# First FFN layer of five groups in 11 instead of 12 products of halves, with the attention one part ahead

One core of a Trainium2 chip. The metric is device microseconds of one execution, median over several; lower is better.

## The reference

Gated linear attention, then a feed-forward layer with a squared ReLU, all FP32 (the weights arrive as 64-bit floats and are converted on the chip).

```python
# q, k, v, alpha: (4, 8, 768, 48)
for t in range(S):
    state = alpha[:, :, t, :, None] * state + einsum('bhd,bhe->bhde', k[:, :, t], v[:, :, t])
    y[:, :, t] = einsum('bhd,bhde->bhe', q[:, :, t], state)
x = y.transpose(0, 2, 1, 3).reshape(3072, 384)
h = maximum(x @ w_in, 0)          # w_in: (384, 2048)
out = (h * h) @ w_out             # w_out: (2048, 384)
```

## The kernel before

The tokens go through in six groups of four blocks of 128. While TensorE does the FFN of group g (`units`), the attention of group g+1 is woven in: each block has four parts (`stages`), and each of the 16 slots of a group takes one attention part and then one sixteenth of the FFN. Groups two to six already use Strassen's seven products for the second layer; the first layer is the plain one. PSUM has four banks for the FFN (`ps_ffn`) and four for the attention.

```python
def ffn_in(g, j):                      # one hidden tile: 128 of 2048 columns, 512 tokens
    ...                                # cut: hid[j // 2] from its pool
    ps = ps_ffn.tile([128, GB * C], FP32, tag="f", name="h")
    for kk in range(KM):               # KM = 3
        nc.tensor.matmul(out=ps, lhsT=w[:, kk, c0 : c0 + 128], rhs=xT[g][:, kk, :],
                         start=(kk == 0), stop=(kk == KM - 1))
    r = p2.tile([128, GB * C], FP32, tag="r", name="r")
    nc.scalar.activation(out=r, in_=ps, func=AF.Relu)
    ...                                # cut: square on ScalarE (first group) or VectorE,
                                       # and four half sums of the hidden tiles on VectorE

stages = [(aT, ln, sn, eb, ei), (qT, mq, kT, mk), (sc, am, kr, kc), (kv, sm, y, ev, st)]
# TensorE: aT qT kT sc kr kv y    ScalarE: ln eb ei kc ev    VectorE: sn mq mk am sm st

for slot in range(NS):                 # NS = 16
    i, s = divmod(slot, len(stages))
    n = (g + 1) * GB + i
    if n < NBLK:
        for f in stages[s]:
            f(n)
    next_weights()
    ...
    while units and done * NS < total * (slot + 1):
        f, args = units.pop(0)
        f(*args)
        done += cost[f]
```

`ev` is twelve ScalarE copies of y out of PSUM into `xT`; `sn` is a scan on VectorE; `eb` and `ei` are exponentials of its result on ScalarE.

## Time and profile before

| | before |
|---|---|
| median (range) of the first runs | 630.0 us (629.78 to 630.14) |
| span of the profiled run (itself one of 632.01 us) | 630.2 us |
| TensorE matmul busy | 616.5 us (98%) |
| VectorE, ScalarE busy | 305.3 us (48%), 224.9 us (36%) |
| first layer, all groups | 576 matmul instructions of 512 columns |

TensorE is the row to read: nearly all of the span, and the chain that ended last is 89% TensorE. The lines themselves stand in the prediction. An FP32 matmul is two instructions here, each with its weight load. "Busy" of a matmul includes a modelled tail, so I measure rates by the distance of starts.

### The profile page before, as it was taken

The numbers are of one execution on the slowest core, as the hardware profiler recorded it, in microseconds if no ns is written. First come the engines' busy times: TensorE is split into PE (matmuls) and PEld (weight loads), VectorE is DVE, ScalarE is ACT, GpSimd is POOL, SyncE is SP. The second block draws the span as 40 slices with busy tenths as digits, with TensorE's granted clock in tenths as the row PEclk, the third lists the DMA queues.
The fourth block names the chain that finished last, engine by engine and source line by source line (L and its number), as shares of the span: only waits on it lengthen the run. The fifth ranks groups of instructions, "written<-read, shape, count | busy, mean of one in ns | idle before, by whom it ended". The sixth has DMA issues, their size and how long they took to land.

```text
span 630.2 us, 8103 instructions
## 1 busy us (share of the span) xinstructions
PE 616.5 (98%) x3284; PEld 438.9 (70%) x3284; DVE 305.3 (48%) x484; ACT 224.9 (36%) x533; POOL 3.8 (1%) x18
## 2 busy tenths in 40 slices
PE   7979999999999999999999999999999999999997
PEld 5745456665556998555899655799854599844797
DVE  5777768674865323555423357523255442145301
ACT  3867784525334123243230443422324403222100
POOL 2000000000000000000000000000000000000000
PEclk8979999999999999999999999999999999999999
DMA  9983755508020201711300802110262000100001
GB/s 155 263 184 102 176 146 127 101 1 143 8 51 14 37 1 54 98 23 29 51 1 25 126 1 50 29 24 2 73 78 50 1 1 1 50 2 0 1 0 51
DMA packets 108709, 36.70 MB, mean 58 GB/s; under 512 B 100480, under 2 KB 103552, under 8 KB 108672
## 3 DMA queue, kind: packets, MB, share of 16 engines
q1 hardware_dynamic: 108672, 36.18, 29.7%
q8 instruction: 26, 0.43, 0.3%
q14 instruction: 11, 0.09, 0.0%
HBM read 31.46 MB, written 4.72 MB: 57 GB/s over the span
## 4 chain that ended last, share of the span: by engine, by line
PE 89%; ACT 5%; DVE 4%; issue 1%; DVEq 0%
PE h L399 36%; PE o L455 29%; PE o L423 6%; PE sc L261 4%; PE y L325 3%; PE y L318 3%; PE kv L290 2%; ACT xT L345 2%; PE kr L279 2%; PE qT L211 1%; PE aT L211 1%; PE kT L211 1%; ACT hid L407 1%; ACT power L137 1%; DVE power L147 1%
## 5 line engine op out<-in xcount | busy, mean ns | idle before, releaser
L399 PE MATMUL h<-xT,w_in 128*128 128x512 f32 x576 | 258.2, 599 | 1.5 <-DVE w_in L154 1.5
L399 PEld LDWEIGHTS h<-xT,w_in 128*128 128x128 f32 x576 | 106.7, 191 | 121.6 <-issue 119.3
L409 DVE TENSOR_TENSOR hid<-r 128x512 f32<-128x512 f32 x80 | 54.8, 691 | 114.7 <-ACT r L404 114.7
L345 ACT COPY xT<-y 32x128 f32<-32x128 f32 (+3 forms) x282 | 72.9, 259 | 102.6 <-PE y L325 97.8
L404 ACT ACTIVATE r<-h 128x512 f32<-128x512 f32 x96 | 56.4, 592 | 114.0 <-PE h L399 113.8
L455 PE MATMUL o<-w_out,hid 128*128 128x192 f32 x480 | 82.0, 327 | 0.0
L455 PEld LDWEIGHTS o<-w_out,hid 128*128 128x128 f32 x480 | 78.1, 190 | 3.1 <-issue 3.1
L455 PE MATMUL o<-t,s 128*128 128x192 f32 x320 | 55.1, 326 | 0.0
L225 DVE TENSOR_TENSOR_SCAN la<-again,la 128x512 f32<-128x512 f32 x24 | 29.3, 1222 | 51.4 <-ACT la L220 51.4
L455 PEld LDWEIGHTS o<-t,s 128*128 128x128 f32 x320 | 52.1, 190 | 0.1
L269 DVE COPY_PREDICATED am<-causal,sc 128x512 f32<-128x512 uint32 x48 | 32.4, 730 | 28.5 <-PE sc L261 28.4
L423 PE MATMUL o<-w_out,hid 128*128 128x384 f32 x128 | 42.9, 489 | 0.3 <-DVE w_out L154 0.3
L423 PEld LDWEIGHTS o<-w_out,hid 128*128 128x128 f32 x128 | 23.7, 190 | 15.7 <-DVE w_out L154 0.5
L261 PEld LDWEIGHTS sc<-qs,ks 48*128 48x128 f32 x384 | 23.8, 191 | 11.2 <-issue 7.4
L284 ACT ACTIVATE kc<-kr 128x512 f32<-128x512 f32 x20 | 11.9, 596 | 49.8 <-PE kr L279 49.8
L234 ACT ACTIVATE b<-la 128x512 f32<-128x512 f32 x24 | 15.1, 630 | 38.7 <-DVE la L225 38.7
L261 PE MATMUL sc<-qs,ks 48*128 48x128 f32 x384 | 28.5, 289 | 0.0
L455 PE MATMUL o<-w_out,s 128*128 128x192 f32 x160 | 27.9, 329 | 0.0
L325 PE MATMUL y<-am,v_in 128*48 128x128 f32 (+1 forms) x384 | 26.5, 278 | 1.4 <-ACT xT L345 1.4
L455 PE MATMUL o<-t,hid 128*128 128x192 f32 x160 | 27.6, 327 | 0.0
L455 PEld LDWEIGHTS o<-w_out,s 128*128 128x128 f32 x160 | 26.0, 190 | 0.7 <-issue 0.7
L455 PEld LDWEIGHTS o<-t,hid 128*128 128x128 f32 x160 | 26.0, 190 | 0.1
(65 smaller groups left out, 498.4 us busy)
## 6 DMA issues: line engine op xcount, KB each, us to landing
raw<-in_moe_w_in_dram SPq DMA_DIRECT2D x8, 768.0 KB, 5.4
raw<-in_moe_w_out_dram SPq DMA_DIRECT2D x8, 768.0 KB, 4.3
a_in<-in_alpha_dram SPq DMA_DIRECT2D x24, 192.0 KB, 4.1
q_in<-in_q_dram SPq DMA_DIRECT2D x24, 192.0 KB, 3.9
k_in<-in_k_dram SPq DMA_DIRECT2D x24, 192.0 KB, 4.4
v_in<-in_v_dram SPq DMA_DIRECT2D x24, 192.0 KB, 4.5
out_dram<-osb SPq DMA_DIRECT2D x24, 192.0 KB, 2.0
```

The lines of the kernel that those rows point to most:

```text
L211: nc.tensor.transpose(out=ps[:, p, :], in_=rows[:, 128 * p : 128 * (p + 1)], identity=ident)
L225: nc.vector.tensor_tensor_scan(out=la.rearrange("a p t -> a (p t)"), data0=again.rearrange("a p t -> a (p t)"), data1=la.rearrange("a p t ...
L261: nc.tensor.matmul(out=ps[e][:, p, :], lhsT=blk[n]["ks"][rows, p, :], rhs=blk[n]["qs"][rows, p, :], start=True, stop=True,)
L269: nc.vector.copy_predicated(out=am_t[n % NAM][:, e], mask=causal.bitcast(U32).unsqueeze(1).to_broadcast([128, NP, C]), data=ps,)
L318: nc.tensor.matmul(out=ys[p // per][:, p % per, :], lhsT=s_t[n % B][:, p, :], rhs=blk[n]["qs"][:, p, :], start=(p % per == 0), stop=False, ...
L325: nc.tensor.matmul(out=ys[p // per][64 * e : 64 * e + D + G * e, p % per, :], lhsT=v_in[:, (2 * p + e) * D - G * e : (2 * p + e + 1) * D], ...
L345: copy(out=xT[g][to : to + m, kk, t * C : (t + 1) * C], in_=ys[p // per][r : r + m, p % per, :],)
L399: nc.tensor.matmul(out=ps, lhsT=w[:, kk, c0 : c0 + 128], rhs=xT[g][:, kk, :], start=(kk == 0), stop=(kk == KM - 1),)
L404: nc.scalar.activation(out=r, in_=ps, func=AF.Relu)
L409: nc.vector.tensor_tensor(out=h, in0=r, in1=r, op=ALU.mult)
L423: nc.tensor.matmul(out=acc[t][:, 0:DM], lhsT=hid[i][:, j, t * C : (t + 1) * C], rhs=w_out[i][:, j, :], start=(i == 0 and j == 0), stop=(i ...
L455: nc.tensor.matmul(out=acc[k][:, t, :], lhsT=lhs[:, j, t * C : (t + 1) * C], rhs=rhs[:, j, :], start=(first and r + j + t == 0), stop=(r = ...
```

## The change

The three row tiles of the contraction (384 = 3 x 128) are taken as two and one. On the first two, Strassen's algorithm over halves (two halves of the hidden columns, two halves of the tokens) needs 7 products of 256 columns instead of 8; the third tile adds its 4. So 11 instead of 12 per pair of hidden tiles. The products go into four PSUM banks, A to D. Strassen's scheme needs running sums of them: ScalarE copies the first product in A to u1, VectorE adds B to it (u2) and C to that (u3). The second products of a pair add to A, C and D, and each must wait until its bank has been read. The sums of the weights are made once, those of x once a group; for this x must be complete earlier, so the attention runs one part ahead. The second layer keeps its products, in another order, and makes its hidden sums in place.

```diff
+    def ffn_in_pair(g, j, part):
+        ...
+        def product(k, *pairs):        # accumulators A, B, C, D: the four banks
+            ...                        # start only at a bank's first matmul of the pair
+        if part == 0:
+            nc.scalar.copy(out=u1, in_=product("A", (a11, b11)))
+            add(u2, product("B", (s2, t2)), u1)
+            add(u3, product("C", (s3, t3), (a23, b32)), u2)
+            add(h2[:, HT : 2 * HT], product("D", (s1, t1)), u3)
+        else:
+            c11 = product("A", (a12, b21), (a13, b31))
+            nc.scalar.activation(out=h1[:, 0:HT], in_=c11, func=AF.Relu)
+            add(h2[:, 0:HT], product("C", (a22, t4), (a23, d3)), u2)
+            add(h1[:, HT : 2 * HT], product("D", (s4, b22), (a13, b32)), u2)
+            ...                        # relu and squares, one hidden sum per two pairs
-            units = [(ffn_in, (g, j)) for j in order]
+            units = [(ffn_in_pair, (g, j, part)) for j in range(NJ // 2) for part in range(2)]
-    PRODUCTS = (("1", 0), ("6", 1), ("2", 0), ("7", 2), ("5", 3), ("4", 2), ("3", 3))
+    PRODUCTS = (("1", 0), ("5", 3), ("6", 1), ("7", 2), ("2", 0), ("4", 2), ("3", 3))
+    stage_ahead(NS)
     for slot in range(NS):
-            if n < NBLK:
-                for f in stages[s]:
-                    f(n)
+            stage_ahead(NS * (g + 1) + slot + 1)
             next_weights()
+            ...                        # cut: weight sums, sums of x in the last slot
```

(Cuts are marked with dots; the moves of helper functions are left out.)

More of the change, by code (lines that the diff above doesn't have):

```diff
@@ L360, in st, with combine, sum_w_in @@
         blk[n].clear()
-    hid, acc, sums = {}, {}, {}
+    hid, acc, ws, xs, sums = {}, {}, {}, {}, {}
     HT, HM, NR2 = GB * C // 2, DM // 2, NJ // 4
-    t1, t2, t4 = (kept(f"t{i}_", NR2, [128, 2, HM]) for i in (1, 2, 4))
-    def sum_weights(r):
+    def combine(steps):
+        for o, x, op, z in steps:
+            nc.vector.tensor_tensor(out=o, in0=x, in1=z, op=op)
+    def sum_w_in(r):
+        if r % 2 == 0:
+            ws["tile"] = raw_pool.tile([128, 6, 256], FP32, tag="raw", name="ws")
+        s1, s2, s4 = ws[r] = [ws["tile"][:, 3 * (r % 2) + i, :] for i in range(3)]
+        a11, a12 = w_in[r][:, 0, :], w_in[r][:, 1, :]
+        a21, a22 = w_in[NR2 + r][:, 0, :], w_in[NR2 + r][:, 1, :]
+        combine((
+            (s1, a21, ALU.add, a22), (s2, s1, ALU.subtract, a11),
+            (a21, a11, ALU.subtract, a21), (s4, a12, ALU.subtract, s2),
+        ))
@@ L371, in sum_weights, with sum_w_out @@
+    tsum = [kept(f"t{i}_", NR2, [128, 2, HM]) for i in (1, 2, 4)]
+    def sum_w_out(i):
+        i, r = divmod(i, NR2)
+        t1, t2, t4 = (t[r] for t in tsum)
         b11, b12 = w_out[r][:, :, 0:HM], w_out[r][:, :, HM:DM]
         b21, b22 = w_out[NR2 + r][:, :, 0:HM], w_out[NR2 + r][:, :, HM:DM]
-        for o, x, z in ((t1, b12, b11), (t2, b22, t1), (t4, b21, t2), (None, b22, b12)):
-            nc.vector.tensor_tensor(
-                out=o[r] if o else b12, in0=x, in1=z if not isinstance(z, list) else z[r],
-                op=ALU.subtract,
-            )
+        o, x, z = ((t1, b12, b11), (t2, b22, t1), (b12, b22, b12), (t4, b21, t2))[i]
+        combine(((o, x, ALU.subtract, z),))
@@ new lines, in sum_x @@
+    def sum_x(g):
+        if not xs:
+            a = raw_pool.tile([128, 3, 2, HT], FP32, tag="raw", name="s012")
+            z = raw_pool.tile([128, 6, HT], FP32, tag="raw", name="s3x")
+            sums.update({r: a[:, r] for r in range(3)})
+            sums[3] = z[:, 0:2, :]
+            xs[0] = [z[:, 2 + i, :] for i in range(4)]
+        t1, t2, t4, d3 = xs[0]
+        (b11, b12), (b21, b22), (b31, b32) = (
+            (xT[g][:, kk, 0:HT], xT[g][:, kk, HT : 2 * HT]) for kk in range(KM)
+        )
+        combine((
+            (t1, b12, ALU.subtract, b11), (t2, b22, ALU.subtract, t1),
+            (b12, b22, ALU.subtract, b12), (t4, b21, ALU.subtract, t2),
+            (d3, b31, ALU.subtract, b32),
+        ))
@@ L379, in halves @@
     def halves(j):
         return hid[j][:, :, 0:HT], hid[j][:, :, HT : 2 * HT]
-    def sum_hidden(r):
-        a11, a21 = halves(r)
-        a12, a22 = halves(NR2 + r)
-        s124 = raw_pool.tile([128, 3, 2, HT], FP32, tag="raw", name="s124")
-        s1, s2, s4 = sums[r] = s124[:, 0], s124[:, 1], s124[:, 2]
-        for o, x, op, z in (
-            (s1, a21, ALU.add, a22), (s2, s1, ALU.subtract, a11),
-            (a21, a11, ALU.subtract, a21), (s4, a12, ALU.subtract, s2),
-        ):
-            nc.vector.tensor_tensor(out=o, in0=x, in1=z, op=op)
@@ L393, in ffn_in, with hidden_tile @@
-    def ffn_in(g, j):
+    def hidden_tile(j):
         if j % 2 == 0:
             hid[j // 2] = hid_pool.tile([128, 2, GB * C], FP32, tag="hid", name="hid")
+        return hid[j // 2][:, j % 2, :]
+    def ffn_in(g, j):
         w, c0 = w_in[j * NW // NJ], j % (NJ // NW) * 128
@@ L402, in ffn_in @@
             )
-        r = p2.tile([128, GB * C], FP32, tag="r", name="r")
+        r = p2.tile([128, 3, HT], FP32, tag="u", name="r")[:, 0:2, :]
         nc.scalar.activation(out=r, in_=ps, func=AF.Relu)
-        h = hid[j // 2][:, j % 2, :]
-        if g == 0:
-            nc.scalar.activation(out=h, in_=r, func=AF.Square)
-        else:
-            nc.vector.tensor_tensor(out=h, in0=r, in1=r, op=ALU.mult)
-            if j >= NJ // 2 and j % 2:
-                sum_hidden(j // 2 - NR2)
+        nc.scalar.activation(out=hidden_tile(j), in_=r, func=AF.Square)
@@ new lines, in ffn_in_pair, with add @@
+    def ffn_in_pair(g, j, part):
+        r, cols = j // 2, slice(j % 2 * 128, j % 2 * 128 + 128)
+        a11, a12, a13 = (w_in[r][:, kk, cols] for kk in range(KM))
+        s3, a22, a23 = (w_in[NR2 + r][:, kk, cols] for kk in range(KM))
+        s1, s2, s4 = (x[:, cols] for x in ws[r])
+        t1, t2, t4, d3 = xs[0]
+        (b11, t3), (b21, b22), (b31, b32) = (
+            (xT[g][:, kk, 0:HT], xT[g][:, kk, HT : 2 * HT]) for kk in range(KM)
+        )
+        def product(k, *pairs):
+            first = k not in acc
+            if first:
+                acc[k] = ps_ffn.tile([128, GB * C], FP32, tag="f", name="h")[:, 0:HT]
+            for i, (a, b) in enumerate(pairs):
+                nc.tensor.matmul(
+                    out=acc[k], lhsT=a, rhs=b, start=(first and i == 0),
+                    stop=(i == len(pairs) - 1), skip_group_check=True,
+                )
+            return acc[k]
+        def add(o, x, z):
+            nc.vector.tensor_tensor(out=o, in0=x, in1=z, op=ALU.add)
+        if part == 0:
+            acc["h"] = hidden_tile(j), hidden_tile(j + NJ // 2)
+            acc["u"] = p2.tile([128, 3, HT], FP32, tag="u", name="u")
+        h1, h2 = acc["h"]
+        u1, u2, u3 = (acc["u"][:, i, :] for i in range(3))
+        if part == 0:
+            nc.scalar.copy(out=u1, in_=product("A", (a11, b11)))
+            add(u2, product("B", (s2, t2)), u1)
+            add(u3, product("C", (s3, t3), (a23, b32)), u2)
+            add(h2[:, HT : 2 * HT], product("D", (s1, t1)), u3)
+        else:
+            c11 = product("A", (a12, b21), (a13, b31))
+            nc.scalar.activation(out=h1[:, 0:HT], in_=c11, func=AF.Relu)
+            add(h2[:, 0:HT], product("C", (a22, t4), (a23, d3)), u2)
+            add(h1[:, HT : 2 * HT], product("D", (s4, b22), (a13, b32)), u2)
+            for k in "ABCD":
+                acc.pop(k)
+            nc.vector.scalar_tensor_tensor(
+                out=h2, in0=h2, scalar=0.0, in1=h2, op0=ALU.max, op1=ALU.mult
+            )
+            nc.scalar.activation(out=h1[:, HT : 2 * HT], in_=h1[:, HT : 2 * HT], func=AF.Relu)
+            nc.scalar.activation(out=h1, in_=h1, func=AF.Square)
+            if j % 2:
+                a21, a22 = halves(r)[1], halves(NR2 + r)[1]
+                combine(((sums[r], a21, ALU.add, a22),))
@@ L444, in ffn_product @@
             acc[k] = ps_ffn.tile([128, 2, HM], FP32, tag="f", name="o")
-        (a11, s3), (a12, a22) = halves(r), halves(NR2 + r)
-        s1, s2, s4 = sums[r]
+        (a11, a21), (a12, a22) = halves(r), halves(NR2 + r)
+        s = sums[r]
+        t1, t2, t4 = (t[r] for t in tsum)
         b11, t3 = w_out[r][:, :, 0:HM], w_out[r][:, :, HM:DM]
@@ L449, in ffn_product @@
         lhs, rhs = {
-            "1": (a11, b11), "2": (a12, b21), "3": (s4, b22), "4": (a22, t4[r]),
-            "5": (s1, t1[r]), "6": (s2, t2[r]), "7": (s3, t3),
+            "1": (a11, b11), "2": (a12, b21), "3": (s, b22), "4": (a22, t4),
+            "5": (s, t1), "6": (s, t2), "7": (a21, t3),
         }[name]
@@ L459, in ffn_product @@
                 )
+        if name == "5":
+            combine(((s, s, ALU.subtract, a11), (a21, a11, ALU.subtract, a21)))
+        elif name == "6":
+            combine(((s, a12, ALU.subtract, s),))
         if r < NR2 - 1:
@@ L467, in ffn_product @@
             nc.scalar.activation(out=acc["u1"], in_=acc[k], func=AF.Copy)
+        elif name == "5":
+            pass
         elif name in "67":
@@ L470, in ffn_product @@
             if new == "u3":
-                acc[new] = p2.tile([128, 2, HM], FP32, tag=new, name=new, bufs=1)
+                acc[new] = acc["out", 1][:, :, HM:DM]
             nc.vector.tensor_tensor(out=acc[new], in0=acc[k], in1=acc[u], op=ALU.add)
+            if new == "u3":
+                nc.vector.tensor_tensor(
+                    out=acc[new], in0=acc[3], in1=acc[new], op=ALU.add
+                )
         else:
-            h, m, u = {"2": (0, 0, None), "5": (1, 1, "u3"), "4": (1, 0, "u2"), "3": (0, 1, "u2")}[name]
+            h, m, u = {"2": (0, 0, None), "4": (1, 0, "u2"), "3": (0, 1, "u2")}[name]
             o = acc["out", h][:, :, m * HM : (m + 1) * HM]
@@ L482, in ffn_product @@
                     store(g, 2 * h + t, acc["out", h][:, t, :])
+            if name == "3":
+                acc.clear()
     stages = [(aT, ln, sn, eb, ei), (qT, mq, kT, mk), (sc, am, kr, kc), (kv, sm, y, ev, st)]
@@ L502, with stage_ahead @@
         steps[f](*([int(rest[0]), rest[1:]] if f == "load" else map(int, rest)))
+    def stage_ahead(i):
+        n, k = divmod(i, len(stages))
+        if n < NBLK:
+            for f in stages[k]:
+                f(n)
+            if k == 0 and n + 1 < NBLK:
+                load(n + 1)
     NS = GB * len(stages)
+    stage_ahead(NS)
     for g in range(NBLK // GB):
         if g:
-            order = [j for r in range(NR2) for i in (r, NR2 + r) for j in (2 * i, 2 * i + 1)]
-            units = [(ffn_in, (g, j)) for j in order]
+            units = [(ffn_in_pair, (g, j, part)) for j in range(NJ // 2) for part in range(2)]
             units += [(ffn_product, (g, i, r)) for i in range(len(PRODUCTS)) for r in range(NR2)]
@@ L513 @@
             units += [(ffn_out, (g, t, i)) for i in range(NW) for t in range(GB)]
-        cost = {ffn_in: KM * GB * C, ffn_out: NJ // NW * DM, ffn_product: 4 * HM}
+        cost = {
+            ffn_in: KM * GB * C, ffn_in_pair: 11 * HT // 2, ffn_out: NJ // NW * DM,
+            ffn_product: 4 * HM,
+        }
         total = sum(cost[f] for f, _ in units)
@@ L517 @@
         for slot in range(NS):
-            i, s = divmod(slot, len(stages))
-            n = (g + 1) * GB + i
-            if n < NBLK:
-                for f in stages[s]:
-                    f(n)
-            next_weights()
-            if g == 1 and slot < NR2:
-                sum_weights(slot)
-            if s == 0 and n + 1 < NBLK:
-                load(n + 1)
+            stage_ahead(NS * (g + 1) + slot + 1)
+            next_weights()
+            if 0 <= g * NS + slot - (NS - 3) < NR2:
+                sum_w_in(g * NS + slot - (NS - 3))
+            if g == 1 and 3 <= slot < 11:
+                sum_w_out(2 * slot - 6)
+                sum_w_out(2 * slot - 5)
+            if slot == NS - 1 and g + 1 < NBLK // GB:
+                sum_x(g + 1)
             while units and done * NS < total * (slot + 1):
```

## The prediction

> **What bounds the kernel now.** I read the busy table and the slices first, then the groups of instructions, then the time line of one stretch in which the first FFN layer and the attention are interleaved.
>
> ```profile
> PE 616.5 (98%) x3284; PEld 438.9 (70%) x3284; DVE 305.3 (48%) x484; ACT 224.9 (36%) x533; POOL 3.8 (1%) x18
> PE   7979999999999999999999999999999999999997
> PEclk8979999999999999999999999999999999999999
> ```
> ```profile
> 60.00:600.00 540.00, 539.33 (x2811) 378.46 (x2812) 260.51 (x411) 186.64 (x449) 0.00 (x0) 1.00 0.24 46
> ```
>
> TensorE is the bound: from 60 to 600 us it shows 539.33 us of work in 540 us (last line, busy times of PE, PEld, DVE and ACT in a window). A busy matmul is not yet one at full rate, so I also took the distance from one matmul's start to the next out of the trace: 0.429 us for a 512-column instruction, 0.1625 us for 192 columns, 0.109 us for 128. After 60 us these distances add up to the time with under 1 us of rest. So TensorE streams without stalls, the two vector engines are half idle, and any column removed is time gained, as long as no stall comes in. Any new stall is time lost, in full.
>
> ```profile
> L399 PE MATMUL h<-xT,w_in 128*128 128x512 f32 x576 | 258.2, 599 | 1.5 <-DVE w_in L154 1.5
> ...
> L404 ACT ACTIVATE r<-h 128x512 f32<-128x512 f32 x96 | 56.4, 592 | 114.0 <-PE h L399 113.8
> ```
> ```profile
> 270.33 3.29 ACT L345 COPY xT<-y 32x128 f32<-32x128 f32 x12 [2.21 <-PE y L325]
> ...
> 273.65 0.60 ACT L404 ACTIVATE r<-h 128x512 f32<-128x512 f32 x1
> ...
> 276.18 0.59 ACT L220 ACTIVATE la<-aT 128x512 f32<-128x512 f32 x1
> ...
> 279.58 1.22 DVE L225 TENSOR_TENSOR_SCAN la<-again,la 128x512 f32<-128x512 f32 x1
> ...
> 280.83 0.63 ACT L234 ACTIVATE b<-la 128x512 f32<-128x512 f32 x1 [4.06 <-DVE la L225]
> ...
> 281.36 0.61 ACT L238 ACTIVATE inv<-la 128x512 f32<-128x512 f32 x1
> ...
> 281.88 1.06 ACT L404 ACTIVATE r<-h 128x512 f32<-128x512 f32 x2
> ```
>
> The first block has two groups, the second lines of the time line (start, length). They show what the reader should keep in mind: ScalarE takes its work strictly in program order. When an attention part puts `ln, exp, exp` or twelve copies (3.29 us) ahead, the ReLU of a finished FFN tile waits: here the tile was ready near 279.1 and its ReLU began at 281.88. TensorE didn't notice, because one tile takes it 6 x 0.429 = 2.57 us and four PSUM buffers let it run three tiles (7.7 us) ahead. That slack is what the change spends.
>
> **What the Trainium skill says.** "TensorE: Matmul & The Clock Gate", section "Back-to-back issue gap", gives an isolated spacing of N/2.4 + 2.5 ns. This trace has twice that per instruction for FP32 (0.429 us at 512), which fits N/1.2 + 2.4 ns, also at 192 and 128; an estimate for 256 columns is thus 0.2158 us. The same page, "Step-by-step: what each phase is for", says matmuls stay in program order and only weight loads are pulled ahead, so a matmul that waits holds up all behind it; the trace agrees (kr, then kv, both waited with the rest behind them). "PSUM — Partial Sum Buffer", section "Engine vs sequencer instructions", says that ScalarE and VectorE are strict first-in first-out; the 281.88 line agrees. The first page's "What's actually happening" has the clock halved after an idle window of about 3.4 us. Here the clock record has windows of 3.413 us, and halves after windows that held 1.12 us (8.1 to 11.5) and 1.04 us (32.0 to 35.4) of streaming; it stays full after one with 1.57 us. So a gap of over some 2 us inside one window may be enough.
>
> **The change part by part.** *Matmuls.* In each of groups two to six, 8 pairs of hidden tiles took 2 x 3 products of 512 columns, at two instructions each: 5 x 8 x 12 = 480 instructions, 480 x 0.429 = 205.9 us. Now each pair has 11 products of 256 columns: 5 x 8 x 22 = 880 instructions x 0.2158 = 189.9 us. Gain **16.0 us**. Weight loads double, but at 128-column matmuls loads keep up with 0.109 us spacing, so they stay hidden. The second layer keeps its 28 x 4 products per group.
>
> *Vector work.* Off the path as a sum: per pair VectorE has five adds of 256 columns (about 0.42 us each, an estimate from 0.691 at 512, 0.558 at 384 and 0.354 at 192) and one of 512 (0.69); before, two squares (1.38) and half of four sums (1.38). ScalarE has three short ones (0.37) and a square (0.63) for two ReLUs (1.18). Both are far under TensorE's 4.75 us a pair.
>
> *Order.* This is the core. A pair's products go A, B, C, C, D (2.16 us), then again into the same accumulators A, A, C, C, D, D (2.59 us). Between them ScalarE must copy A (u1), and VectorE must add B (u2), C (u3), D, each needing the one before. The second A overwrites what the copy reads, so TensorE waits for it: the slack is 1.73 us from the end of A, instead of 7.7 us. The built order puts exactly one attention part and then one pair in each slot, and that part's ScalarE and VectorE work goes ahead of u1 and u2. I work it out for each kind, with 0 as the moment TensorE has issued the previous pair's last product. Handoffs of 0.035 us, and 0.165 us for the matmul's tail, are from the trace. The previous pair's tail is: D lands 0.17, VectorE add to 0.62, its ReLU-square of the other half to 1.23; ScalarE ReLU to 1.03, square to 1.69.
>
> Pair after aT (two per group, four groups): `ln` 1.60 to 2.19, scan 2.23 to 3.45, `exp` 3.48 to 4.11, second `exp` to 4.63, u1 to 4.91; the matmul restarts at about 5.0. TensorE had aT (0.44) and the first five products (2.16), so it stood ready at 2.60. Stall **2.4 us** x 8 = 19.2.
>
> Pair after kv and y (two per group, four groups): these take TensorE 2.9 us; the twelve copies begin when y lands, 3.0, and last to 6.3; u1 to 6.62, restart 6.75. TensorE was ready at 2.9 + 2.16 = 5.06. Stall **1.7 us** x 8 = 13.6.
>
> Pair after qT and kT in the middle of the layer (one per group, four groups): VectorE has the hidden sum to 2.42, then mq and mk to 3.61, u2 to 3.97, u3 to 4.42. The second C needs u3, and TensorE is there at 0.87 + 2.16 + 0.86 = 3.9. Stall 0.65 x 4 = 2.6.
>
> Pair after sc and kr: kc on ScalarE to 2.39, u1 to 2.67, TensorE there at 3.75; u3 is ready at 3.93 and needed at 4.6. No stall.
>
> Group two also carries the weight sums on VectorE: some 1.5 us. Group six has no attention: u1 is ready when needed, and the sum after every second pair makes u3 late by some 0.5 us: with the group's start about 2 us.
>
> *Clock.* A gap of 2.4 us lying nearly whole in one 3.413 us window leaves it with about 1 us of streaming; the chance is about (3.41 - 2.4 + 0.4)/3.41 = 0.4. Each halved window costs 1.7 us: 8 x 0.4 x 1.7 = 5.5, **say 6 us**; the shorter stalls leave over 1.6 us and shouldn't do it.
>
> *Attention one part ahead.* It frees the slot in which the sums of x are made and takes away two waits of 0.5 us at 72 and 100 us; in group one it moves mq and mk ahead of a weight conversion. Net about 0.
>
> *Second layer.* Its in-place sums come after product 5: 4 x 1.4 us on VectorE, and product 6 needs the last of them about 9 us after product 5 began; they finish near 7, or 8.4 with an attention part between. No stall.
>
> Sum: 630.0 - 16.0 + 19.2 + 13.6 + 2.6 + 1.5 + 2.0 + 6.0 = 658.9; I say **658 us**, slower.
>
> **The rivals.** (a) *Work bound*: the stalls hide, and the 16 us come through: 614 us, 2.5% faster. For it speaks that TensorE is at 98% and the vector engines at about half. Against it: an average says nothing on latency, and ScalarE's queue alone keeps u1 back by 3 to 4 us in half of the attention slots. With half of my stalls it would be about 635. (b) *Stalls without the clock*: the waits come as worked out, but the clock stays full: 653 us. (c) *VectorE as the new bound*: if the 256-column adds cost like 512-column ones, a pair has 5 x 0.69 + 0.69 + 0.35 = 4.5 us, with attention more than TensorE's slot in places; the pairs after qT would stall by 2 us more, and the second C, not the second A, would be the usual wait: about 670 us. The near straight line through 192, 384 and 512 speaks against it. (d) *Weight loads bind at 256 columns*: 880 x 0.24 would eat the gain; the 192-column group at 0.1625 speaks against it.
>
> **Range and chances.** The surest term is the 16.0 us; the stalls of 39 us may be off by a third (26 to 50), the clock from 0 to 10. Together 642 to 672 us, 8 times in 10. Slower by over 2% means over 642.6; within 2% needs stalls of some 4 to 28 us in all, which would take my handoffs to be wrong in kind; faster needs nearly none. Chances: faster 0.04, same 0.07, slower 0.89.
>
> **What would show it.** Right: 880 first-layer matmuls with starts 0.216 us apart where nothing waits; TensorE idle after 60 us in pieces of about 2.4 us (released by the ScalarE copy u) in the pairs after aT, about 1.7 us after kv and y, none after sc; some half-clock windows right after the former; PE busy below 95%. Group six without attention should gain about 1 us over its old length. Wrong: PE still near 98% and the span near 614 (the copy isn't what the second A waits for, or ScalarE is free sooner); waits ended by VectorE's u3 as the larger share (rival c); even spacing of 0.24 us or more without waits (rival d); stalls in the second layer.

## The result

| | before | after |
|---|---|---|
| median (range) | 629.89 us (629.24 to 630.14) | 666.31 us (662.04 to 667.1) |
| span of the profiled run | 630.2 us | 664.0 us |
| mean granted clock of that run | 0.991 | 0.982 |

All outputs are right. The ratio is 1.0566 (95% interval 1.052 to 1.0612): 5.7% slower. Ratios are the mean time of one kernel's fast runs over that of the other's of the same rounds, so not quite the ratio of the medians quoted.

The page of the changed kernel, its busy table and two rows of the slices, and then the window of 60 to 600 us (busy times of PE, PEld, DVE, ACT):

```profile
PE 615.7 (93%) x3684; PEld 515.7 (78%) x3684; DVE 375.3 (57%) x685; ACT 247.9 (37%) x613; POOL 3.8 (1%) x18
PE   7799999998888999988899979799998989999997
PEclk9989999999898999989999989999998989999999
```
```profile
60.00:600.00 540.00, 505.63 (x3023) 426.45 (x3022) 306.54 (x565) 197.87 (x497) 0.00 (x0) 0.98 0.22 45
```

Where TensorE had 539.33 us of work in 540 us it now has 505.63: gaps of 34 us. And the clock row, full after the start before, now has single slices at 8 in the middle. Who TensorE waited for, in the view of waits (total us, times, longest):

```profile
PE h L449 <- ACT u L464: 29.1, 16, 2.2
PE h L449 <- DVE u L456: 3.9, 8, 1.5
```

Sixteen waits for one instruction, the ScalarE copy u1; this is what half of the 32 pairs of groups two to five do. (This view counts idle time from a matmul's modelled end; by distances of starts the sixteen are eight of 1.6 us and eight of 2.4 us, 31.7 us in all.) The time line shows one of each kind. First a pair after kv and y (start, length):

```profile
273.88 3.28 ACT L345 COPY xT<-y 32x128 f32<-32x128 f32 x12 [1.29 <-PE y L325]
277.18 0.37 ACT L464 COPY u<-h 128x256 f32<-128x256 f32 x1
```
```profile
275.59 0.59 PE L449 MATMUL h<-s3x,ws 128*128 128x256 f32 x2
277.61 1.13 PE L449 MATMUL h<-xT,w_in 128*128 128x256 f32 x4 [1.43 <-ACT u L464]
```

A's first product was done near 274.5, but u1 could not start before 277.18, behind the twelve copies. The line at 275.59 is D, the last product that needs no u1; then TensorE waits to 277.61. The next pair, after aT:

```profile
280.43 0.60 PE L211 MATMUL aT<-ident,a_in 128*128 128x128 f32 x4
...
281.54 0.63 ACT L479 ACTIVATE hid<-hid 128x512 f32<-128x512 f32 x1
...
282.07 0.58 ACT L220 ACTIVATE la<-aT 128x512 f32<-128x512 f32 x1
...
282.60 0.59 PE L449 MATMUL h<-s3x,ws 128*128 128x256 f32 x2
282.68 1.22 DVE L225 TENSOR_TENSOR_SCAN la<-again,la 128x512 f32<-128x512 f32 x1 [1.03 <-ACT la L220]
283.94 0.63 ACT L234 ACTIVATE b<-la 128x512 f32<-128x512 f32 x1 [1.29 <-DVE la L225]
284.48 0.61 ACT L238 ACTIVATE inv<-la 128x512 f32<-128x512 f32 x1
285.00 0.35 ACT L464 COPY u<-h 128x256 f32<-128x256 f32 x1
...
285.40 1.74 PE L449 MATMUL h<-xT,w_in 128*128 128x256 f32 x4 [2.21 <-ACT u L464]
```

It is the same queue again: ScalarE sits idle for 1.29 us with u1's input ready, since the exponential ahead of u1 waits for VectorE's scan. At 285.79 the clock is halved for one window, so the four matmuls from 285.40 take 1.74 us instead of the 1.13 us of those at 277.61.

### The profile page after: what moved, and what is told of

Same layout as the page of the kernel before. It is cut to its first block, busy times and chain, and to the rows that moved or that the text cites. A ratio compares the mean times of both kernels' runs of the same rounds, so it can differ in the third digit from the quotient of the medians.

```text
span 664.0 us, 9283 instructions
## 1 busy us (share of the span) xinstructions
PE 615.7 (93%) x3684; PEld 515.7 (78%) x3684; DVE 375.3 (57%) x685; ACT 247.9 (37%) x613; POOL 3.8 (1%) x18
## 4 chain that ended last, share of the span: by engine, by line
PE 76%; ACT 13%; DVE 8%; issue 2%; DVEq 0%
PE o L528 28%; PE h L449 25%; PE o L494 6%; ACT xT L345 6%; PE sc L261 4%; PE y L325 3%; PE y L318 2%; DVE la L225 2%; PE kv L290 2%; PE kr L279 2%; PE qT L211 1%; PE kT L211 1%; ACT b L234 1%; ACT la L220 1%; ACT hid L479 1%
## 5 line engine op out<-in xcount | busy, mean ns | idle before, releaser
L449 PE MATMUL h<-xT,w_in 128*128 128x256 f32 x480 | 135.1, 394 | 29.1 <-ACT u L464 29.1
L456 DVE TENSOR_TENSOR hid<-h,u 128x256 f32<-128x256 f32 x120 | 51.0, 425 | 64.6 <-PE h L449 60.4
L456 DVE TENSOR_TENSOR u<-h,u 128x256 f32<-128x256 f32 x80 | 33.9, 424 | 44.1 <-ACT u L464 36.6
L449 PE MATMUL h<-s3x,w_in 128*128 128x256 f32 x160 | 48.4, 429 | 3.9 <-DVE u L456 3.9
L478 ACT ACTIVATE hid<-hid 128x256 f32<-128x256 f32 x40 | 16.7, 417 | 87.5 <-DVE hid L456 87.5
L449 PE MATMUL h<-s3x,ws 128*128 128x256 f32 x160 | 47.6, 379 | 0.0
L425 PE MATMUL h<-xT,w_in 128*128 128x512 f32 x96 | 42.9, 596 | 2.4 <-DVE w_in L154 2.4
L449 PEld LDWEIGHTS h<-s3x,w_in 128*128 128x128 f32 x160 | 31.2, 207 | 15.5 <-DVE u L456 11.5
L470 ACT ACTIVATE hid<-h 128x256 f32<-128x256 f32 x40 | 15.3, 383 | 67.5 <-PE h L449 67.5
L449 PEld LDWEIGHTS h<-s3x,ws 128*128 128x128 f32 x160 | 30.4, 190 | 4.1
```

What stands on the lines that cost most here:

```text
L449: nc.tensor.matmul(out=acc[k], lhsT=a, rhs=b, start=(first and i == 0), stop=(i == len(pairs) - 1), skip_group_check=True,)
L456: nc.vector.tensor_tensor(out=o, in0=x, in1=z, op=ALU.add)
L470: nc.scalar.activation(out=h1[:, 0:HT], in_=c11, func=AF.Relu)
L478: nc.scalar.activation(out=h1[:, HT : 2 * HT], in_=h1[:, HT : 2 * HT], func=AF.Relu)
```

## The experiments

Two batches, on two chips, each beside runs of the kernel before (medians 630.15 and 630.28 us). All edits are to the changed kernel, unless said.

### e1: all vector work of the attention behind the first half of a pair

In a slot the attention part's matmuls stay where they are; its ScalarE and VectorE instructions are emitted after part 0 of the pair.

```diff
+    TENSOR = (aT, qT, kT, sc, kr, kv, y)
+    LATE = (0, 1, 2, 3)
     def stage_ahead(i, pair_next=False):
             for f in stages[k]:
-                f(n)
+                if pair_next and k in LATE and f not in TENSOR:
+                    later.append((f, n))
+                else:
+                    f(n)
     ...
                 f, args = units.pop(0)
                 f(*args)
+                for h, n in later:
+                    h(n)
+                later = []
```

> The changed kernel, with the ScalarE and VectorE work of each attention part moved in program order behind the first half (A, B, C, C, D and u1, u2, u3) of the pair that follows it. No instruction is added or taken away. Theory (queue order: u1 waits behind the attention part's work, and the second A waits for u1): the sixteen stalls of 1.6 and 2.4 us (32 us), most of the stalls after qT (about 5 us) and all clock drops in the interleaved groups (six halved windows, 10 us) go; span about 630 - 16 + 3 = 617 us, at most 622. Rival 1 (256-column instructions, doubled weight loads or the longer accumulation groups cost the time): they are all still there, so the time stays near 664. Rival 2 (VectorE is the new bound): its work is the same, so at most a small part goes, above 650.

Measured: 619.86 us (616.55 to 620.1), ratio 0.9813 (0.978 to 0.9846). The view of waits has no wait for ScalarE's u1 left, and four short ones for VectorE's u:

```profile
PE h L449 <- DVE u L456: 1.0, 4, 0.4
```

The time line of ScalarE in the pair after aT:

```profile
269.42 0.35 ACT L464 COPY u<-h 128x256 f32<-128x256 f32 x1
269.68 0.60 ACT L220 ACTIVATE la<-aT 128x512 f32<-128x512 f32 x1
272.46 0.63 ACT L234 ACTIVATE b<-la 128x512 f32<-128x512 f32 x1 [2.19 <-DVE la L225]
273.00 0.61 ACT L238 ACTIVATE inv<-la 128x512 f32<-128x512 f32 x1
```

ScalarE still waits for the scan, longer than before (2.19 us), but u1 is through, and nobody needs the exponentials yet. The same instructions on the same engines, in another order, make the 664.0 us span 617.9 us. (Against the kernel before, the gain of 1.9% is clear of noise, but whether it reaches 2% is not: the interval spans 0.98.) That rules out the narrower matmuls, the doubled weight loads and VectorE's load as the cause of the loss (rivals c and d of the prediction). Distances of starts agree: the median between 256-column instructions is 0.216 us in the changed kernel too.

### e2 and e3: one kind of part alone

e2 is e1 with `LATE = (0,)` (ln, scan, two exps), e3 with `LATE = (3,)` (kv, y, twelve copies).

> As the run before, for the parts with ln, scan and two exps alone. Theory: eight stalls of 2.4 us go (19.2 us), and since only these left a clock window with under 1.2 us of streaming, all six halved windows go too (10.2 us): about 664 - 29 = 635 us, with the 1.6 us stalls after kv and y still there and the clock at full throughout the interleaved groups. If the clock drops have another cause (the 1.6 us stalls, or the mean load), some stay and the time is 638 to 645.

> As e1, for the parts with kv, y and the twelve copies alone. Theory: eight stalls of 1.6 us go (12.7 us), the 2.4 us stalls and about six halved clock windows stay: about 664 - 13 = 651 us. Rival: if the 1.6 us stalls had a share in the halved windows, these fall in number and the time is under 648.

Measured: e2 637.64 us (636.33 to 638.82), ratio 1.0106; e3 649.8 us (645.15 to 654.03), ratio 1.0287. Waits of e2, then of e3:

```profile
PE h L449 <- ACT u L464: 11.4, 8, 1.4
PE h L449 <- DVE u L456: 4.5, 8, 1.6
```
```profile
PE h L449 <- ACT u L464: 17.7, 8, 2.2
PE h L449 <- DVE u L456: 3.9, 8, 1.5
```

Each move took away its own eight waits and left the other eight. (e2 is 2.6 us over its figure; its profiled run has four halved windows at the start where that of the changed kernel has one, which may be a part of it.) And the clock, the same row of the slices of e2, then of e3:

```profile
PEclk8979999999999999999999999999999999999999
```
```profile
PEclk8979999999898999989999999899998999999999
```

With the short stalls alone (e2) no window is halved after the start; with the long ones alone (e3) six are. So in these runs the clock follows the 2.4 us stalls and not the 1.6 us ones. How many windows fall changes from run to run: e3's four timed runs went from 645.15 us at a mean clock of 0.992 to 654.03 us at 0.974, the changed kernel's from 662.04 us at 0.987 to 667.1 us at 0.977. This fits the scatter of these two, 5 to 9 us where the kernel before scatters by under 3; that the count depends on where the windows lie is argued, since only one run of each was traced.

### e4: the kernel before with the attention one part ahead alone

```diff
+    stage_ahead(NS)
             for slot in range(NS):
-            if n < NBLK:
-                for f in stages[s]:
-                    f(n)
+            stage_ahead(NS * (g + 1) + slot + 1)
```

> The kernel before, with only the attention one part ahead (12 products, 512 columns, old order of the second layer). Theory: this part of the change is neutral, 629 to 631 us, perhaps 1.6 us more from a wait for a weight conversion near 65 us. Rival: the shift itself puts attention work at worse places and costs several us or more.

Measured: 630.56 us (630.49 to 630.75), ratio 0.9995 (0.9973 to 1.0017). This part of the change is neutral. The wait for a weight conversion near 66 us (1.6 us) and one of 0.5 us near 93 us did come.

### e6: the second half in the order C, D, A

```diff
-            c11 = product("A", (a12, b21), (a13, b31))
-            nc.scalar.activation(out=h1[:, 0:HT], in_=c11, func=AF.Relu)
             add(h2[:, 0:HT], product("C", (a22, t4), (a23, d3)), u2)
             add(h1[:, HT : 2 * HT], product("D", (s4, b22), (a13, b32)), u2)
+            c11 = product("A", (a12, b21), (a13, b31))
+            nc.scalar.activation(out=h1[:, 0:HT], in_=c11, func=AF.Relu)
```

> The changed kernel with the second half of a pair in the order C, C, D, D, A, A instead of A, A, C, C, D, D. Rival: the wait is for the reuse of bank A while ScalarE reads it; then moving the second A to the end takes the sixteen stalls away, about 625 us. Theory: the wait is for the chain that begins at u1, and A is only where it is first felt; the second C then waits for u3, 0.95 us later (u2 and u3 at 0.42 us each and handoffs), so the stalls grow to about 3.3 and 2.5 us, other pairs get small ones, more clock windows are halved: 685 to 705 us.

Measured: 701.38 us (698.11 to 702.72), ratio 1.1129. The stalls are 3.2 us after aT and 2.6 us after kv and y, and the one releaser is now a VectorE add. In the pair after aT near 295 us the two adds u2 and u3 end at 295.32 us and TensorE restarts at 295.38 us, with the second C, so it is u3, the add that reads C:

```profile
PE h L449 <- DVE u L456: 55.5, 29, 3.0
```

So the bank that TensorE comes to first is only where the wait is felt. What is late is the chain u1, u2, u3, and the later its link, the longer the wait. The author's order, A first, is the best of these two.

### e7: u1 on VectorE

```diff
-            nc.scalar.copy(out=u1, in_=product("A", (a11, b11)))
+            nc.vector.tensor_copy(out=u1, in_=product("A", (a11, b11)))
```

> The changed kernel with one line changed: the copy u1 is made by VectorE (a 256-column copy, some 0.4 us) instead of ScalarE; the attention's work stays where it is. Theory (u1 waits in ScalarE's queue): after kv and y VectorE isn't held up by the twelve copies, so those eight stalls of 1.6 us go altogether; after aT VectorE's queue holds the scan, but not the two exps, so these stalls fall from 2.4 to about 1.4 us and no window is halved. Against it 0.4 us more wait for u3 in the pairs after qT and in group six (some 3 us). About 664 - 13 - 8 - 10 + 3 = 636 us. Rival (VectorE is the bound): 40 more instructions on it make the time longer than 664.

Measured: 641.75 us (640.57 to 642.89), ratio 1.0176. The stalls after kv and y are gone, those after aT are 1.3 us in groups three to five, and no window is halved after the start. One changed line, which moves work to the fuller engine, wins some 25 us over the changed kernel (666.31 to 641.75 us, in different batches). My figure missed by 6 us: in group two the weight sums on VectorE stand ahead of u1 and make waits of 2.2, 1.9 and 2.2 us, the pairs after qT wait 1.0 us, and group six has three waits of 0.7 us; the queue of VectorE has the same fault at other places.

```profile
PE h L449 <- DVE u L464: 17.1, 16, 2.0
```

### e5: e1 with two more moves

```diff
+            if not g:
+                next_weights()             # group one: conversions ahead of the attention part
             later = stage_ahead(...)
-            next_weights()
+            if g:
+                next_weights()
     # in ffn_in_pair, the hidden sum of an odd pair:
-                combine(((sums[r], a21, ALU.add, a22),))
+                pending.append((sums[r], a21, ALU.add, a22))   # done after the next pair's D add
```

> e1 with two more moves: in group one the weight conversion of a slot is put ahead of its attention part (against the 1.6 and 0.5 us waits near 65 and 95 us), and the hidden sum of an odd pair is put behind the next pair's u1, u2, u3 (against the 0.4 to 0.6 us waits of u3, 1.7 us together). Theory: e1 less about 3 us, so 615 to 617 us, under the kernel before by some 2.2%. If the weights ahead delay mq, mk or the copies so that TensorE waits elsewhere, nothing is won, 619 to 621 us.

Measured: 616.99 us (615.19 to 617.68), ratio 0.9779 (0.9753 to 0.9806): faster than both kernels, 2.2% under the one before (the interval spans 0.98 here too). In the window of 60 to 600 us TensorE is full again:

```profile
60.00:600.00 540.00, 539.90 (x3290) 467.29 (x3289) 324.39 (x611) 206.89 (x523) 0.00 (x0) 1.00 0.22 45
```

One new wait stands outside this window: near 48 us the matmuls of sc wait 1.6 us for VectorE's ks, which now comes behind the weight conversion. The intervals of e1 and e5 overlap and they ran in different batches, so their times don't show that e5 is the faster of the two. The traces do, by 2.0 us: their last matmuls start at 613.7 and 611.7 us, and the first 256-column ones at 149.7 and 149.1 us.

## Why the prediction was right

It said 658 us, slower; measured were 666.31 us, inside the range. (The terms add up to 658.9.) The cause was right, and so were the places and lengths of the stalls; the 8 us that it fell short lie mostly in the clock and in short delays for which it had no term. Term by term, with what the runs showed:

- *Matmuls, 16.0 us gained.* Right in kind. From one matmul's start to the next, the first layer of groups two to six took 207.9 us before (what all 512-column instructions after 56 us took, less the 64 of group one at 0.434 us). It took 242.9 us in the changed kernel, 194.4 us in e1 and 193.0 us in e5. So the saving that exists is 13.5 to 14.9 us; the rest of the 16.0 goes into remaining waits and small handovers to the attention. The 242.9 us of the changed kernel are 190.1 us of streaming, 37.5 us of waits over 0.25 us, 9.2 us of halved clock and 6.2 us of delays under 0.25 us. The prediction had 38.9 us for the waits, 6 for the clock and nothing for the short delays. These are mostly 0.1 us each: for one, the first matmul after a wait takes 0.32 us instead of 0.216, and so does the first of the second C soon after. The kernel before has 1.9 us of such delays in its first layer and e5 2.9 us, so about half of the 6.2 came with the stalls. The spacing of 0.2158 us held (0.216), weight loads did not bind.
- *Stalls after aT, 2.4 us x 8 = 19.2.* Measured eight of 2.4 us; e2 removes them.
- *Stalls after kv and y, 1.7 us x 8 = 13.6.* Measured eight of 1.6 us; e3 removes them.
- *Stall after qT in the middle of the layer, 0.65 us x 4 = 2.6, and group two's weight sums, 1.5.* Measured 0.7 us in groups three to five and 1.6 us in group two, and 0.5 us at that group's start.
- *Group six, about 2 us.* Measured three of 0.4 us. This was the term that was too large; the group's first layer went from 41.2 to 39.9 us, where about 1 us had been said.
- *None after sc and kr.* None seen.
- *Clock, 6 us.* The mechanism was right, the size was not: six of the eight long stalls were followed by a halved window in the profiled run, not three, and by distances of starts these cost 9.2 us in the first layer, 1.5 us each. I had taken the chance as 0.4 by asking that the gap lie nearly whole in one window; the record shows that a window with up to 1.3 us of streaming already does it, so about 2.1 of the 2.4 us are enough. That lifts the chance only to about 0.5 (an estimate: (3.41 - 2.38 + 2 x 0.28) / 3.41), or four of eight; that it was six may be luck in where the windows lay, which wasn't tested. So the kernel became 36.4 us longer where 28 had been said, and of the 8.4 us between them the first layer shows 6.1: 3.2 from the clock, 4.3 from short delays (6.2 less the 1.9 of before), less 1.4 for the waits. Another 0.9 is the rounding of the sum; the rest was not traced.
- *Attention one part ahead, net about 0.* e4: 630.56 against 630.15 us.
- *Second layer, no stall.* None seen in any run.
- *A misreading.* In the kernel before, the tile whose ReLU began at 281.88 us was ready at 278.66, when its last matmul ended, not near 279.1. It waited 3.2 us; the conclusion is the same.

Rival (a), that the stalls hide because the vector engines are half idle, is refuted by the waits and by e1. Rival (b), a full clock, is refuted by the clock row. Rival (c) would have given waits for u3 in the main and no cure by a change of order. Rival (d) is refuted by the spacing.

What is not shown: I did not hold the clock up in the changed kernel without removing the stalls, so its 9.2 us are read from distances of starts in the halved windows, not from a run of their own. e2 and e7 show only that with no 2.4 us stall left no window is halved between the start and the end.

## What to carry to other kernels

Before you swap a matmul schedule with deep buffers for one that feeds results back into its own accumulators, work out how long TensorE can run before it needs the first answer (here 7.7 us before, 1.73 us after), and compare this with the longest run of work that stands ahead of the answer in the answering engine's queue; mean load says nothing about it. If the queue is too long, emit the short urgent instruction first: e1 changed no instruction, only their order, and turned a loss of 5.7% into a gain of 1.9%. A bubble of over 2 us on TensorE can cost more than itself: after six of the eight stalls of 2.4 us here, the clock of the next window was halved.

## What the Trainium skill lacked or had wrong

- "TensorE: Matmul & The Clock Gate", "Back-to-back issue gap": its warm formula N/2.4 + 2.5 ns has no FP32 form. "FP8 and Floating Point Precision", "TensorE Precision Notes", counts four passes for true FP32, but gives no spacing. The runs show two instructions per FP32 matmul, at 0.429 us (512 columns), 0.216 us (256) and 0.1625 us (192) each, so N/1.2 + 2.4 ns; two instructions at twice the page's N/2.4 agree with the four passes.
- The same page, "What's actually happening": it has the clock halved after an idle window of some 3.4 us, and a later table warns of gaps over about 3 us. For shorter gaps it gives no length. Here six of eight gaps of 2.4 us were enough. Between 60 and 600 us of all nine traces, every window of 3.413 us with up to 1.31 us of streaming was followed by a halved one, and every one with 1.46 us or more by a full one. At a kernel's start and end there are exceptions, such as a halved window after 1.58 us at the start of e3 and a full one after 1.28 us at the end of e4.
- The same page says that the window is free-running. The runs fit that, with a consequence that the page numbers only for a kernel's start: the changed kernel lost 5 to 9 windows' worth of half clock from run to run (mean clock 0.987 to 0.977, worked out over its span), 662 to 667 us.
- "Perfetto Trace Analysis", "Identifying the Most-Contended Engine": occupancy alone would not lead to ScalarE here, which at 37% held TensorE back for 31.7 us. The page's advice under "Optimization Strategy", to find the gaps and who ends them, is what found it.
